# One level of Strassen's method in the first matrix product of a fused attention and gated-MLP kernel

## The chip, the cores and the metric

The kernel runs on one core of a Trainium2 chip. The metric is the device time of one execution in microseconds (us), taken as the median of several runs.

## The reference

For each of 4 batches there is a channel attention over 6080 tokens of 256 channels, and its output goes through an MLP of width 2048. In short (tau is 1.0):

```python
qn = q / (np.linalg.norm(q, axis=1, keepdims=True) + 1e-06)
kn = k / (np.linalg.norm(k, axis=1, keepdims=True) + 1e-06)
s = kn.transpose(0, 2, 1) @ qn / tau          # 256 x 256 per batch
a = softmax(s)
x = (v @ a).reshape(B * S, D)                 # 24320 tokens x 256
h = x @ w_in                                  # 2048 columns
g = h * (1.0 / (1.0 + np.exp(-1.702 * h)))
out = g @ w_out
```

q, k and v are float32; the weights w_in and w_out arrive as 64-bit floats and are turned into float32 on the chip.

## The kernel before

The attention matrix is folded into the weights: per batch W = a @ w_in (256 x 2048) is computed once, and the first product is v @ W. Every float32 operand of a large product is held as two tiles of a rounded format (F32R), a high part and a low part: `split` (lines 77-80) makes the high part with a copy on ACT (the cast of line 78) and the low part with a subtraction on DVE (line 79). One product is three matmuls: high by high, high by low, low by high.

A batch has 12 chunks of tokens: 11 of 512 and one of 448. W has 16 blocks of 128 columns (f = 0 to 15). For each chunk and each block, `hidden` (line 456) makes h for 128 columns and 512 tokens: two halves of the 256 channels (j) times three matmuls, so 6 matmuls of 512 columns into one PSUM bank `ps_h` (line 466). ACT takes the gate out of PSUM (line 473, tile g), makes gh (line 78), and DVE makes gl (line 79). Two to three steps later `project` (line 484) multiplies by w_out: 2 halves of the output times 3 matmuls, again 6 matmuls of 512 columns (line 494), summed over the 16 blocks in two PSUM banks `ps_o`. One step of the loop over (chunk, block) is thus 12 matmuls.

Between the steps lies other work, given by a table of due steps (`put`, lines 641-689): the next chunk of v is loaded and split (`v_load`, `v_split`, tiles v_h and v_l); the next batch's q and k are split (qs, ks), squared and summed for the norms (sq on ACT, acc on POOL, lines 240-243) and multiplied to scores (lines 288 and 297, the latter matmuls of 256 columns) every four steps; and before a batch ends its W is made (`weights`, line 406, four groups of four blocks). In the first batch w_in and w_out are also converted (lines 121-135) while two chunks run side by side. PE's order is written out by hand; the other engines' order comes from a scheduler, and each engine then works through its queue strictly in that order.

## Time and profile before

| what | value |
|---|---|
| time, 3 runs | 2280.66 us median (2280.4 to 2280.85) |
| the profiled execution's own time | 2280.42 us |
| its span in the profile | 2278.6 us |
| PE (matmul) | busy 2272.3 us, 100% of the span, 10256 matmuls |
| ACT | busy 1233.9 us, 54% |
| DVE | busy 904.8 us, 40% |
| POOL | busy 221.0 us, 10% |

A row of the groups by line reads: line, engine, operation, tile written <- tiles read, shape, count, then busy us and mean ns of one, then the idle time of the engine ahead of them and who ended it. In the timeline a row gives start, duration, engine, line and operation; xN merges N instructions. Matmuls are pipelined, so a matmul's duration is longer than the distance to the next one: the distance of two starts is what a matmul costs in a row.

### The profile page before, as it was taken

To read this page: it belongs to the slowest core of one execution; us is meant where nothing else is said; L and a number is where in the kernel's file an instruction comes from. 1 tells how busy PE (TensorE), PEld (TensorE's weight loads), DVE (VectorE), ACT (ScalarE), POOL (GpSimd) and SP (SyncE) were. 2 spreads that over 40 slices of the span, in tenths; PEclk is the share of its full clock that TensorE was granted. 3 is DMA by queue.
4 is the path that set the end of the run, shared out by engine and by line. 5 is a ranking of instruction groups with operands and counts; after the bars stand their busy time and mean duration, and the time that the engine had idled before them with its cause. 6 is when DMAs were issued, how large, how long until landed. Compare 5 with 4: busy or idle time off the path is not lost.

```text
span 2278.6 us, 26628 instructions
## 1 busy us (share of the span) xinstructions
PE 2272.3 (100%) x10256; PEld 1902.0 (83%) x10256; DVE 904.8 (40%) x1305; ACT 1233.9 (54%) x2146; POOL 221.0 (10%) x168
## 2 busy tenths in 40 slices
PE   9999999999999999999999999999999999999999
PEld 8888888888888888888888888888888888888888
DVE  7754444433334444443333444444333223223222
ACT  7765555554455555555545555555454445444444
POOL 0022222000002222200000222220000000000000
PEclk9999999999999999999999999999999999999999
DMA  9312111100011211110000121210001000000000
GB/s 367 93 47 65 65 56 54 56 18 19 20 36 56 74 56 56 63 47 18 19 28 27 61 70 56 66 44 19 18 19 36 19 19 32 25 19 29 27 10 18
DMA packets 45520, 109.72 MB, mean 48 GB/s; under 512 B 4432, under 2 KB 7248, under 8 KB 45392
## 3 DMA queue, kind: packets, MB, share of 16 engines
q1 hardware_dynamic: 45392, 108.02, 14.1%
q8 instruction: 80, 1.31, 0.2%
q14 instruction: 48, 0.39, 0.1%
HBM read 83.10 MB, written 24.90 MB: 47 GB/s over the span
## 4 chain that ended last, share of the span: by engine, by line
PE 99%; DVE 0%; DMA 0%; SPq 0%; issue 0%; ACT 0%; DVEq 0%
PE ps_h L466 46%; PE ps_o L494 45%; PE s L288 3%; PE ps_w L420 2%; PE s L278 2%; PE s L297 1%; DMA raw_k<-in_k 0%; PE ps_n L315 0%; PE s_first L253 0%; SPq L207 0%; DVE v_l L85 0%; PE ps_t L392 0%; PE ps_b L340 0%; DVE wl L79 0%; DVE m L367 0%
## 5 line engine op out<-in xcount | busy, mean ns | idle before, releaser
L473 ACT ACTIVATE g<-ps_h 128x512 f32<-128x512 f32 (+1 forms) x768 | 455.6, 593 | 945.1 <-PE ps_h L466 937.7
L79 DVE TENSOR_TENSOR gl<-g,gh 128x512 fp32r<-128x512 f32 (+1 forms) x768 | 591.6, 772 | 942.0 <-ACT gh L78 941.7
L466 PE MATMUL ps_h<-v_h,wh 128*128 128x512 f32 (+1 forms) x1536 | 596.8, 389 | 0.0
L466 PE MATMUL ps_h<-v_l,wh 128*128 128x512 f32 (+1 forms) x1536 | 595.5, 388 | 0.0
L466 PE MATMUL ps_h<-v_h,wl 128*128 128x512 f32 (+1 forms) x1536 | 594.7, 387 | 0.2 <-DVE wl L79 0.2
L494 PE MATMUL ps_o<-gh,wo_l 128*128 128x512 f32 (+1 forms) x1536 | 594.7, 387 | 0.0
L494 PE MATMUL ps_o<-gh,wo_h 128*128 128x512 f32 (+1 forms) x1536 | 594.7, 387 | 0.0
L494 PE MATMUL ps_o<-gl,wo_h 128*128 128x512 f32 (+1 forms) x1536 | 594.5, 387 | 0.0
L78 ACT CAST gh<-g 128x512 fp32r<-128x512 f32 (+1 forms) x768 | 472.7, 615 | 20.5
L466 PEld LDWEIGHTS ps_h<-v_h,wl 128*128 128x128 f32 x1536 | 288.3, 188 | 58.2 <-DVE wl L79 0.6
L494 PEld LDWEIGHTS ps_o<-gh,wo_l 128*128 128x128 f32 x1536 | 288.4, 188 | 57.1
L494 PEld LDWEIGHTS ps_o<-gh,wo_h 128*128 128x128 f32 x1536 | 288.3, 188 | 57.1
L494 PEld LDWEIGHTS ps_o<-gl,wo_h 128*128 128x128 f32 x1536 | 288.3, 188 | 56.7
L466 PEld LDWEIGHTS ps_h<-v_h,wh 128*128 128x128 f32 x1536 | 288.7, 188 | 54.8
L466 PEld LDWEIGHTS ps_h<-v_l,wh 128*128 128x128 f32 x1536 | 288.7, 188 | 54.4
L243 POOL TENSOR_TENSOR acc_q<-acc_q,sq 128x512 f32<-128x512 f32 (+1 forms) x72 | 90.0, 1251 | 1245.9 <-ACT sq L241 1245.9
L79 DVE TENSOR_TENSOR qs<-raw_q,qs 128x512 fp32r<-128x512 f32 (+1 forms) x71 | 47.6, 670 | 212.8 <-ACT qs L78 210.0
L243 POOL TENSOR_TENSOR acc_k<-acc_k,sq 128x512 f32<-128x512 f32 (+1 forms) x72 | 117.8, 1636 | 0.2
L79 DVE TENSOR_TENSOR v_l<-v_raw,v_h 128x512 fp32r<-128x512 f32 (+1 forms) x92 | 65.1, 748 | 79.1 <-ACT v_h L78 79.1
L288 PE MATMUL s<-qs,ks 128*128 128x512 f32 x272 | 73.2, 389 | 0.0
L241 ACT ACTIVATE sq<-raw_k 128x512 f32<-128x512 f32 (+1 forms) x96 | 57.9, 604 | 6.2 <-DMA raw_k<-in_k 3.4
L241 ACT ACTIVATE sq<-raw_q 128x512 f32<-128x512 f32 (+1 forms) x96 | 58.8, 613 | 2.1 <-DMA raw_q<-in_q 2.1
(92 smaller groups left out, 860.2 us busy)
## 6 DMA issues: line engine op xcount, KB each, us to landing
v_raw<-in_vT SPq DMA_DIRECT2D x44, 512.0 KB, 3.8
out_T<-osb SPq DMA_DIRECT2D x88, 256.0 KB, 2.1
raw_q<-in_q SPq DMA_DIRECT2D x43, 512.0 KB, 3.7
raw_k<-in_k SPq DMA_DIRECT2D x43, 512.0 KB, 4.4
words<-in_w_in SPq DMA_DIRECT2D x8, 512.0 KB, 8.0
words<-in_w_out SPq DMA_DIRECT2D x8, 512.0 KB, 3.4
v_raw<-in_vT SPq DMA_DIRECT2D x4, 448.0 KB, 3.6
out_T<-osb SPq DMA_DIRECT2D x8, 224.0 KB, 2.0
```

The source lines that it names most:

```text
L78: ins = nc.scalar.copy(dst_hi, src)
L79: nc.vector.tensor_tensor(dst_lo, src, dst_hi.bitcast(F32), op=ALU.subtract)
L241: nc.scalar.activation(sq, r, AF.Square)
L243: eng.tensor_tensor(acc, acc, sq, op=ALU.add)
L278: nc.tensor.matmul(self.s[i][:, :C], lhsT=ks[:, j, i * P : (i + 1) * P], rhs=qs[:, j, :], start=u == start and j == 0, stop=last and j == ...
L288: nc.tensor.matmul(self.s[i], lhsT=ks[:, j, 0, i * P : (i + 1) * P], rhs=qs[:, j, :, :], start=u == start and j == 0, stop=False, skip_gro ...
L297: nc.tensor.matmul(self.s[i][:, C:], lhsT=ks[:, j, 1, i * P : (i + 1) * P], rhs=qs[:, j, 0, :], start=False, stop=last and j == nt - 1, sk ...
L420: nc.tensor.matmul(ps, lhsT=l[:, j, ci], rhs=r[:, j, :], start=n == 0, stop=n == 3 * NC2 - 1,)
L466: nc.tensor.matmul(ps[:, :w], lhsT=l[:, j, fs], rhs=r[:, j, :w], start=n == 0, stop=n == 3 * NC2 - 1,)
L473: newest[0] = nc.scalar.activation(g, ps[:, :w], AF.Gelu_apprx_sigmoid)
L494: nc.tensor.matmul(out[d][:, :w], lhsT=l[:, f, ds], rhs=r[:, :w], start=f == 0 and n == 0, stop=f == NF - 1 and n == 2,)
```

## The change

`hidden` becomes a class, `Hidden`, which works on a pair of blocks of W's columns (fp = 0 to 7) and on the two halves of a chunk (256 tokens each, 224 in the short chunk). With the two halves of the channels this is a 2 by 2 by 2 product of blocks: eight block products in the plain way, seven by Strassen's method (in Winograd's form). Each block product is three matmuls of 256 columns, so a pair of blocks takes 21 matmuls of 256 columns, where two calls of `hidden` took 12 of 512. `project` is unchanged.

The seven products need seven combinations of the blocks of W and of v. For v, `v_load` now makes three transfers, `v_sums` makes four sums or differences of 128x256 (on POOL, but on DVE for the first three chunks), and `v_split` splits seven parts of 256 columns (as 512, 512, 512 and 256) instead of two of 512. For W, the product is copied out of PSUM by ACT, `weight_sums` makes four sums (on POOL, in the first batch on DVE), and `weight_split` splits seven blocks instead of four.

The results are put together in two PSUM banks, ps_x and ps_y, in three stages. `begin`: two products; ACT copies the first to r1 (L553), DVE adds it to the second: u2 (L554). `middle`: two products; DVE adds r25 (L561) and then adds r25 into ps_y (L563). `end`: three products added into the banks; DVE adds u2 into ps_x (L569) and into ps_y (L570), then the two gates follow (L581) with gh and gl. In PE's order `end` of a pair comes right ahead of `begin` of the next: 15 matmuls of 256 columns, then a `project` of 6 of 512, then `middle` (6 of 256), then a `project` of 6 of 512, then the next `end`. By the waits in the built program the first matmul of `middle` waits for u2, its fourth for r1, the first of `end` for r25, and the seventh of `end` for the sum of L563.

Room is found by other means: ps_h has 4 banks and ps_o 2 (before 3 and 3), the float32 w_in goes to DRAM and is loaded again per group, the squares have 2 buffers instead of 4, and several tiles share room. The work between the steps has new due steps, and W of the next batch is made in the last chunk and the first steps after it.

```diff
-    ps_h = ctx.enter_context(tc.tile_pool(name="ps_h", bufs=3, space=PSUM))
-    ps_o = ctx.enter_context(tc.tile_pool(name="ps_o", bufs=3, space=PSUM))
+    ps_h = ctx.enter_context(tc.tile_pool(name="ps_h", bufs=4, space=PSUM))
+    ps_o = ctx.enter_context(tc.tile_pool(name="ps_o", bufs=2, space=PSUM))
...
-                    sq = sp.tile([P, UT, C], F32, tag="sq", name="sq", bufs=4)[:, :nt, :]
+                    sq = sp.tile([P, UT, C], F32, tag="sq", name="sq", bufs=2)[:, :nt, :]
...
+        def spare(self, i, name):
+            if self.alone:
+                return ps_h.tile([P, NCH], F32, tag="h", name=name)
+            return ps_s.tile([P, NCH], F32, tag=f"s{i}", name=name)
...
+        def win_load(self, g):
+            win[g] = sp.tile([P, NC2, GW], F32, tag="win", name="win", bufs=1)
+            nc.sync.dma_start(win[g], parts[g])
         def win_split(self, g, step=split):
             self.win_h = sp.tile([P, NC2, GW], F32R, tag="qs", name="win_h")
             self.win_l = sp.tile([P, NC2, GW], F32R, tag="ks", name="win_l")
-            return step(self.win_h, self.win_l, win[:, :, g * GW : (g + 1) * GW])
+            if self.alone:
+                parts[g] = dram.tile([P, NC2, GW], F32, name=f"win{g}")
+                nc.sync.dma_start(parts[g], win[g])
+            return step(self.win_h, self.win_l, win[g])
...
-            return split(self.wh[g][:, i, :], self.wl[g][:, i, :], ps)
...
+            src = ps.rearrange("p (q f n) -> p f q n", q=2, f=2)
+            for f in range(2):
+                nc.scalar.copy(self.wf[0][:, ((0, 3), (1, 2))[i][f]], src[:, f])
+        def weight_sums(self, g):
+            t, u = self.wf
+            eng = nc.vector if self.alone else nc.gpsimd
+            eng.tensor_tensor(u[:, 1], t[:, 0], t[:, 3], op=ALU.subtract)
+            eng.tensor_tensor(t[:, 3], t[:, 3], t[:, 2], op=ALU.add)
+            eng.tensor_tensor(u[:, 0], t[:, 3], t[:, 0], op=ALU.subtract)
+            eng.tensor_tensor(u[:, 2], t[:, 1], u[:, 0], op=ALU.subtract)
+        def weight_split(self, g, part):
+            if part == 0:
+                self.wh[g] = wp.tile([P, 7, 2, P], F32R, tag=f"wh{g}", name="wh")
+                self.wl[g] = wp.tile([P, 7, 2, P], F32R, tag=f"wl{g}", name="wl")
+            o = slice(*((0, 4), (4, 7))[part])
+            split(self.wh[g][:, o], self.wl[g][:, o], self.wf[part])
...
+        early = b == 0 and c < 2
+        room = [(wp, f"{t}{1 + c}") if early else (cv, "words") for t in ("wh", "wl")]
+        t, u = (
+            pool.tile([P, n, NCH // 2], F32, tag=tag, name="v_raw")
+            for n, (pool, tag) in zip((4, 3), room)
+        )
+        vraw[b, c] = (t, u)
+        src = vT[b, :, o : o + w].rearrange("(c p) (h n) -> p c h n", p=P, h=2)
+        nc.sync.dma_start(t[:, 1:3, :hw], src[:, 1])
+        nc.sync.dma_start(t[:, 0, :hw], src[:, 0, 0])
+        nc.sync.dma_start(t[:, 3, :hw], src[:, 0, 1])
+    def v_sums(b, c):
+        hw = chunks[c][1] // 2
+        t, u = (x[:, :, :hw] for x in vraw[b, c])
+        eng = nc.vector if b == 0 and c < 3 else nc.gpsimd
+        eng.tensor_tensor(u[:, 1], t[:, 2], t[:, 3], op=ALU.subtract)
+        eng.tensor_tensor(t[:, 3], t[:, 3], t[:, 0], op=ALU.subtract)
+        eng.tensor_tensor(u[:, 0], t[:, 2], t[:, 3], op=ALU.subtract)
+        eng.tensor_tensor(u[:, 2], t[:, 1], u[:, 0], op=ALU.subtract)
+    def v_split(b, c, part, step=split):
+        hw = chunks[c][1] // 2
+        if part == 0:
+            vparts[b, c] = [
+                vp.tile([P, 7, NCH // 2], F32R, tag=t, name=t) for t in ("vh", "vl")
+            ]
+        n = 4 if b == 0 and c < 2 else 2
+        o = slice(2 * part, min(2 * part + n, 7))
+        i = slice(2 * part % 4, 2 * part % 4 + (o.stop - o.start))
+        h, l = (x[:, o, :hw] for x in vparts[b, c])
+        return step(h, l, vraw[b, c][part // 2][:, i, :hw])
...
-    def hidden(at, b, c, f):
-        w = chunks[c][1]
-        vh, vl = vsplit[b, c]
-        grp, o = divmod(f, FG)
-        fs = slice(o * P, (o + 1) * P)
-        wh, wl = at.wh[grp], at.wl[grp]
-        ps = ps_h.tile([P, NCH], F32, tag="h", name="ps_h")
-        n = 0
-        for j in range(NC2):
-            for l, r in ((wh, vh), (wh, vl), (wl, vh)):
...
+    class Hidden:
+        def __init__(self, at, b, c, fp):
+            self.b, self.c, self.fp = b, c, fp
+            self.hw = chunks[c][1] // 2
+            self.w = [x[fp // 2][:, :, fp % 2, :] for x in (at.wh, at.wl)]
+            self.v = vparts[b, c]
+        def product(self, out, wi, vi, first=False, last=False):
+            (wh, wl), (vh, vl) = self.w, self.v
+            for n, (l, r) in enumerate(((wh, vh), (wh, vl), (wl, vh))):
                 nc.tensor.matmul(
-                    ps[:, :w], lhsT=l[:, j, fs], rhs=r[:, j, :w],
-                    start=n == 0, stop=n == 3 * NC2 - 1,
+                    out, lhsT=l[:, wi, :], rhs=r[:, vi, : self.hw],
+                    start=first and n == 0, stop=last and n == 2,
+                    skip_group_check=True,
                 )
-                n += 1
-        g = gp.tile([P, NCH], F32, tag="g", name="g")[:, :w]
-        newest[0] = nc.scalar.activation(g, ps[:, :w], AF.Gelu_apprx_sigmoid)
-        there = wide[0] and wide[0] % 5 < 2
-        gh = (cv if there else gp).tile([P, NCH], F32R, tag="z" if there else "gh", name="gh")
-        gl = (cv if there else gp).tile([P, NCH], F32R, tag="low" if there else "gl", name="gl")
-        wide[0] += wide[0] > 0
-        split(gh[:, :w], gl[:, :w], g)
-        return gh, gl
+        def begin(self):
+            hw = self.hw
+            x, y = (ps_h.tile([P, NCH], F32, tag="h", name=nm) for nm in ("ps_x", "ps_y"))
+            self.x = x[:, : 2 * hw].rearrange("p (h n) -> p h n", h=2)
+            self.y = y[:, : 2 * hw].rearrange("p (h n) -> p h n", h=2)
+            self.product(self.x[:, 0], 0, 0, first=True)
+            self.product(self.y[:, 1], 4, 4, first=True)
+            r1, u2 = (
+                gp.tile([P, NCH // 2], F32, tag=tag, name=nm, bufs=2)[:, :hw]
+                for nm, tag in (("r1", "r"), ("u2", "u2"))
+            )
+            self.u2 = u2
+            newest[0] = nc.scalar.copy(r1, self.x[:, 0])
+            nc.vector.tensor_tensor(u2, self.y[:, 1], r1, op=ALU.add)
+        def middle(self):
+            hw = self.hw
+            self.product(self.y[:, 0], 5, 5)
+            self.product(self.x[:, 1], 3, 3)
+            r = gp.tile([P, NCH // 2], F32, tag="r", name="r25", bufs=2)[:, :hw]
+            nc.vector.tensor_tensor(r, self.x[:, 1], self.u2, op=ALU.add)
+            nc.vector.tensor_tensor(self.y[:, 1], self.y[:, 0], r, op=ALU.add)
+        def end(self):
+            self.product(self.x[:, 0], 1, 1, last=True)
+            self.product(self.x[:, 1], 6, 2, last=True)
+            self.product(self.y[:, 0], 2, 6, last=True)
+            nc.vector.tensor_tensor(self.x[:, 1], self.x[:, 1], self.u2, op=ALU.add)
+            nc.vector.tensor_tensor(self.y[:, 0], self.y[:, 0], self.u2, op=ALU.add)
+            return [
+                (self.b, self.c, 2 * self.fp + n, *self.gate(ps))
+                for n, ps in enumerate((self.x, self.y))
+            ]
...
+        def gate(self, ps):
+            w = 2 * self.hw
+            ps = ps.rearrange("p h n -> p (h n)")
+            g = gp.tile([P, NCH], F32, tag="g", name="g", bufs=2)[:, :w]
+            nc.scalar.activation(g, ps, AF.Gelu_apprx_sigmoid)
...
+            for s, (c, fp) in enumerate(order):
+                if b == 0 and 2 * s == WIDE:
+                    wide[0] = 1
+                if open_:
+                    late.extend(open_.pop().end())
+                h = Hidden(at, b, c, fp)
+                open_.append(h)
+                h.begin()
+                if len(late) > 2:
+                    project(*late.pop(0))
+                sides(2 * s)
+                h.middle()
+                if len(late) > 2:
+                    project(*late.pop(0))
+                sides(2 * s + 1)```

The order on two engines at a seam between chunks shows what the scheduler made of it. On ACT, before, the splitting of v (v_h) stands between a gate and its gh, in the last batch:

```order
L473 ACTIVATE g<-ps_h 128x512
L78 CAST v_h<-v_raw 128x512 x2
L78 CAST gh<-g 128x512
L473 ACTIVATE g<-ps_h 128x512
L78 CAST gh<-g 128x512
```

After, at the same seam (r_... is r1 of a pair, ps_x and ps_y are its two banks):

```order
L553 COPY r_24263<-ps_x 128x256
L581 ACTIVATE g<-ps_y 128x512
L82 CAST gh<-g 128x512 x2
L82 CAST vh<-v_raw 128x512 x3
L82 CAST vh<-v_raw 128x256
L581 ACTIVATE g<-ps_x 128x512
L553 COPY r_24321<-ps_x 128x256
L581 ACTIVATE g<-ps_y 128x512
```

The four casts of v now stand ahead of the gate of a pair's ps_x and of the next pair's r1. By the waits in the built program, the first of them waits for the last matmul of `end` of the last pair of the chunk whose vh and vl are overwritten (there are two buffers of each).

On DVE, before:

```order
L79 TENSOR_TENSOR gl<-g,gh 128x512 x13
L79 TENSOR_TENSOR v_l<-v_raw,v_h 128x512 x2
L79 TENSOR_TENSOR gl<-g,gh 128x512 x3
L502 COPY osb<-ps_o 128x512
L79 TENSOR_TENSOR gl<-g,gh 128x512 x13
```

After, the two pairs around the same seam (u_... is u2, r_... beside ps_x is r25 or r1):

```order
L554 TENSOR_TENSOR u_24264<-ps_y,r_24263 128x256
L83 TENSOR_TENSOR gl<-g,gh 128x512 x2
L561 TENSOR_TENSOR r_24281<-ps_x,u_24264 128x256
L563 TENSOR_TENSOR ps_y<-ps_y,r_24281 128x256
L569 TENSOR_TENSOR ps_x<-ps_x,u_24264 128x256
L570 TENSOR_TENSOR ps_y<-ps_y,u_24264 128x256
L83 TENSOR_TENSOR vl<-v_raw,vh 128x512 x3
L83 TENSOR_TENSOR vl<-v_raw,vh 128x256
L554 TENSOR_TENSOR u_24322<-ps_y,r_24321 128x256
L83 TENSOR_TENSOR gl<-g,gh 128x512
```

DVE has six kinds of work in a pair where it had one, and at the seam the four subtractions of v stand between a pair's last sum and the next pair's u2. Such a group of four stands on both engines once per chunk, 46 times in the program.

More of the change, by code (lines that the diff above doesn't have):

```diff
@@ L178, in __init__ @@
             short = UT if self.alone else 0
-            self.loads = [(t, RT) for t in range(short, T + 1, RT)]
+            self.rt = 6 if self.alone else RT
+            self.loads = [(t, self.rt) for t in range(short, T + 1, self.rt)]
             if short:
@@ L387, in transposes @@
             self.aT_l = small.tile([P, NC2, C], F32R, tag="aT_l", name="aT_l")
-            ps = ps_h.tile([P, NCH], F32, tag="h", name="ps_t")
+            ps = self.spare(0, "ps_t")
             psv = ps.rearrange("p (c x) -> p c x", c=NC2)
@@ L611, in channel_attention_then_glu @@
     for s, (what, n) in begun.items():
-        if s > 2:
+        if (what, n) not in (("in", 3), ("out", 1)):
             put0(s - 3, fetch[what], n)
```

174 lines of the change are left out of this document (95 added, 79 removed).

## The prediction

> **What bounds the kernel now.** I read the page first: the busy shares, the granted clock and the chain that ended last.
>
> ```profile
> span 2278.6 us, 26628 instructions
> PE 2272.3 (100%) x10256; PEld 1902.0 (83%) x10256; DVE 904.8 (40%) x1305; ACT 1233.9 (54%) x2146; POOL 221.0 (10%) x168
> PEclk9999999999999999999999999999999999999999
> PE 99%; DVE 0%; DMA 0%; SPq 0%; issue 0%; ACT 0%; DVEq 0%
> PE ps_h L466 46%; PE ps_o L494 45%; PE s L288 3%; PE ps_w L420 2%; PE s L278 2%; PE s L297 1%; DMA raw_k<-in_k 0%; PE ps_n L315 0%; PE s_first L253 0%; SPq L207 0%; DVE v_l L85 0%; PE ps_t L392 0%; PE ps_b L340 0%; DVE wl L79 0%; DVE m L367 0%
> ```
>
> PE is the bound in every stage, at full clock, and half of its time is the product that the change rewrites. So any matmul time saved there is saved from the end, unless PE then has to wait. What a matmul costs in a row is the distance of two starts; the timeline of PE beside a score step of batch 1 shows both sizes.
>
> ```profile
> 880.08 0.39 PE L466 MATMUL ps_h<-v_h,wh 128*128 128x512 f32 x1
> ...
> 885.30 0.39 PE L494 MATMUL ps_o<-gh,wo_l 128*128 128x512 f32 x1
> 885.52 1.07 PE L288 MATMUL s<-qs,ks 128*128 128x512 f32 x4
> 886.43 0.64 PE L297 MATMUL s<-qs,ks 128*128 128x256 f32 x4
> 886.90 0.40 PE L466 MATMUL ps_h<-v_h,wh 128*128 128x512 f32 x1
> ...
> 888.06 0.39 PE L466 MATMUL ps_h<-v_h,wl 128*128 128x512 f32 x1
> ```
>
> From 880.08 to 885.52 lie the 24 matmuls of two steps: 5.44 us, 0.227 each. The four of 256 columns take 886.43 to 886.90: 0.1175 each, not half of 0.227. And the five of 512 that follow them take 888.06 - 886.90 = 1.16, 0.232 each: a little is given back after a run of short ones.
>
> **The matmuls: what goes and what comes.** For a pair of blocks, 24 matmuls of 512 (5.44) become 21 of 256 and 12 of 512 in two runs of six. 21 x 0.1175 = 2.47; each run of six is five at 0.232 and one at 0.227, 1.39, twice 2.77. The pair takes 5.24: 0.20 less. There are 4 x 11 x 8 = 352 such pairs, 70 us. The 32 pairs of the short chunks scale about as their columns, 0.18 each, 6 us. Sum: -76 us. The bounds: four short ones are few, and 0.47 is rounded, so 0.12 may stand for 0.1175 (21 x 0.0025 = 0.05 a pair, -57 us in all); if nothing is given back after them (0.227 all through), 0.05 more, -95 us.
>
> The Trainium skill, "TensorE: Matmul & The Clock Gate", section "Back-to-back issue gap", puts the warm distance at N/2.4 + 2.5 ns: 109 ns for 256 columns and 216 for 512. By that a pair would save 12 x 216 - 21 x 109 = 0.30 us, an estimate of 115 us in all; this trace disagrees on both sizes (0.1175 and 0.227), and the rows decide.
>
> **Whether PE can keep that pace.** Before, ACT and DVE only waited for PE. Now PE waits for them four times a pair, so I walk through a pair by hand. Durations come from the groups by line and shape, distances on one engine from the timeline.
>
> ```profile
> L79 DVE TENSOR_TENSOR gl<-g,gh 128x512 fp32r<-128x512 f32 x704 | 551.7, 785 | 850.1 <-ACT gh L78 849.8
> L297 PE MATMUL s<-qs,ks 128*128 128x256 f32 x272 | 43.7, 281 | 0.0
> L297 PEld LDWEIGHTS s<-qs,ks 128*128 128x128 f32 x272 | 42.0, 189 | 5.5
> L79 DVE TENSOR_TENSOR win_l<-win,win_h 128x1024 fp32r<-128x1024 f32 x15 | 19.2, 1277 | 6.6 <-ACT win_h L78 6.6
> L78 ACT CAST win_h<-win 128x1024 fp32r<-128x1024 f32 x15 | 15.7, 1049 | 1.6 <-PE s L297 0.8 <-DVE win L135 0.7
> L361 DVE TENSOR_TENSOR x<-s,x 128x256 f32<-128x256 f32 x6 | 2.3, 417 | 0.7 <-ACT x L360 0.7
> L360 ACT COPY x<-s 128x256 f32<-128x256 f32 x4 | 1.3, 376 | 1.4 <-PE s L297 1.4
> ```
>
> ```profile
> 1002.21 0.39 PE L466 MATMUL ps_h<-v_h,wl 128*128 128x512 f32 x1
> ...
> 1002.64 0.60 ACT L473 ACTIVATE g<-ps_h 128x512 f32<-128x512 f32 x1 [1.47 <-PE ps_h L466]
> ...
> 1003.27 0.62 ACT L78 CAST gh<-g 128x512 fp32r<-128x512 f32 x1
> ...
> 1003.92 0.69 DVE L79 TENSOR_TENSOR gl<-g,gh 128x512 fp32r<-128x512 f32 x1 [2.03 <-ACT gh L78]
> ...
> 1005.36 0.60 ACT L473 ACTIVATE g<-ps_h 128x512 f32<-128x512 f32 x1 [1.47 <-PE ps_h L466]
> ...
> 1005.85 1.13 ACT L78 CAST v_h<-v_raw 128x512 fp32r<-128x512 f32 x2
> ...
> 1006.49 1.30 DVE L79 TENSOR_TENSOR v_l<-v_raw,v_h 128x512 fp32r<-128x512 f32 x2 [1.88 <-ACT v_h L78]
> ...
> 1006.88 0.62 ACT L78 CAST gh<-g 128x512 fp32r<-128x512 f32 x1
> ```
>
> A gate takes 0.60, a cast 0.62, a subtraction of 512 0.69; whoever waits starts 0.03 to 0.04 after the end. Work that needn't wait starts earlier: the next cast 0.49 after a gate (1005.36, 1005.85), 0.515 after a cast (two in 1.03), the next subtraction 0.61 after one (1.30 - 0.69); I take 0.1 off a copy and 0.08 off an add in the same way, 0.27 and 0.33. A sum out of PSUM of 256 is L361, 0.417; r1 is L360, 0.376; a matmul of 256 ends 0.28 after its start.
>
> Count from the first matmul of `end` of the pair before. `end` lasts 1.06, `begin` until 1.76, `project` until 3.15: there `middle` is due. It lasts until 3.86, the second `project` until 5.24: there the next `end` is due. L569 can start at 0.91 (its product's last start 0.59, and 0.28 + 0.04), L570 at 1.26. ACT: gate of ps_x 1.37, r1 1.86 to 2.24, gate of ps_y 2.13, gh 2.62 to 3.24 and 3.14 to 3.76. DVE: u2 2.27 to 2.69, so `middle` is met with 0.4 to spare; gl 3.27 and 3.88, r25 4.49 to 4.91 (its product is done at 4.06), so `end` is met with 0.3 to spare; L563 until 5.36, due only at 5.95. An ordinary pair keeps PE's pace.
>
> **The seam between chunks.** It doesn't, by the same walk, where v is split. The first cast of vh waits for the last matmul of `end`: 1.26. Then ACT has the casts at 1.26, 1.78, 2.29 and 2.81, the gate at 3.08 and r1 at 3.57 to 3.95. DVE's four subtractions stand at 1.91, 2.52, 3.13 and 3.74, then u2 from 4.07 to 4.49. `middle` is due at 3.15 and can start at 4.53: 1.38 late. Either queue alone makes it late (r1 alone: u2 at 3.98). Before, nobody on PE waited for what is queued behind these casts. What a wait costs beyond itself shows where PE waits for a weight split in the first steps:
>
> ```profile
> 59.42 0.50 PE L466 MATMUL ps_h<-v_h,wl 128*128 128x512 f32 x1 [0.15 <-DVE wl L79]
> 59.76 0.40 PE L466 MATMUL ps_h<-v_h,wh 128*128 128x512 f32 x1
> ```
>
> The next one comes 0.34 later, not 0.23: 0.11 more. So 1.49 a seam; 45 of the 46 groups lie outside the first steps: +67 us. Bounds: 1.28 if only r1 is late (58), 1.9 if the subtractions also meet POOL (86).
>
> **The other added work.** *POOL beside DVE.* The subtractions are slower while POOL works:
>
> ```profile
> 890.79 1.29 POOL L243 TENSOR_TENSOR acc_q<-acc_q,sq 128x512 f32<-128x512 f32 x1 [9.29 <-ACT sq L241]
> 891.71 0.92 DVE L79 TENSOR_TENSOR gl<-g,gh 128x512 fp32r<-128x512 f32 x1 [0.78 <-ACT gh L78]
> 892.04 1.73 POOL L243 TENSOR_TENSOR acc_k<-acc_k,sq 128x512 f32<-128x512 f32 x1
> 892.86 1.47 DVE L79 TENSOR_TENSOR gl<-g,gh 128x512 fp32r<-128x512 f32 x1 [0.23 <-ACT gh L78]
> ```
>
> 0.92 and 1.47 instead of 0.69. Where the next batch's q and k are prepared (every second pair, 68 times by the 272 matmuls of L297), ACT's two casts and two squares push gh to 4.70; a gl of 1.47 then ends at 6.82, and the following sums and u2 at 8.44, where `middle` is due at 8.39: 0.1 late, 0.2 with the restart. Where the gl takes 0.69 nothing is late. v's four sums on POOL add such a meeting once a chunk, 0 to 0.3. Together 0 to 27 us; I take 12. The Trainium skill, "SBUF — State Buffer", section "Who interferes with whom", says that a DVE instruction contends with a POOL read only if both its inputs are in SBUF, so the new sums out of PSUM would be spared; no row here has one beside POOL.
>
> *W of the next batch*, 12 groups: 1.75 times the split, in `win_h`-sized pieces (1.05 on ACT, 1.28 on DVE) beside the gates. The walk gives u2 about 0.5 late once a group, with the restart 0.6: +7, between 0 and 18.
>
> *The first 16 pairs*, where DVE also converts the weights:
>
> ```profile
> 58.00:75.00 17.00, 16.85 (x75) 13.63 (x74) 15.08 (x26) 12.52 (x22) 0.00 (x0) 1.00 0.30 94
> 75.00:97.00 22.00, 22.00 (x98) 18.19 (x97) 15.61 (x27) 15.91 (x27) 0.00 (x0) 1.00 0.31 96
> 97.00:120.00 23.00, 23.00 (x103) 18.97 (x101) 16.39 (x27) 15.96 (x27) 0.00 (x0) 1.00 0.31 92
> 120.00:146.00 26.00, 26.00 (x116) 21.48 (x115) 13.10 (x21) 16.97 (x31) 2.53 (x2) 1.00 0.00 1
> ```
>
> DVE (fourth figure of time) works 60 of these 88 us. Added are 80 sums of 0.417 (33), three groups of W (4 sums and 0.75 of a split more, 7) and one group of v (2): 102, less 0.08 for each of some 200 neighbours, 86 at best. So DVE is full there, and PE gains nothing: I take 98, +10 against the 88, between -3 and +20; the 3 us of savings that the sum counts for them are within that.
>
> *Before the first product* the new path from W in PSUM is two copies (0.65), three sums in a row (1.35), a cast of 1.05 and a subtraction of 1.28, 4.3, against 0.6 + 0.7: +3, between 0 and 6. At the end, the last two gates lie behind four `project`s' worth of matmuls as before: nothing.
>
> **Sum.** -76 + 67 + 12 + 7 + 10 + 3 = +23 on the profiled execution's 2280.42 (its span 2278.6 and 1.8 around it; 0.24 under the median of 2280.66): 2303 us. With all terms at their ends the case reaches from 2240 (-95 + 58 - 3) to 2380 (-57 + 86 + 27 + 18 + 20 + 6).
>
> **Rivals.** *The seam is hidden (faster).* Both engines have room (DVE 40%, ACT 54%), and the walk fails at one place only. If `middle` isn't held there, 67 us go: 2236. It decides as soon as a seam costs under (76 - 32)/45 = 0.98 us. Against it: two queues, each late by itself.
>
> *Long runs of short matmuls are cheaper than four of them (faster).* At half of 0.227, a pair saves 12 x 0.227 - 21 x 0.1135 = 0.34, 131 us with the short chunks as full ones: 2280 - 131 + 99 = 2248. Against it: the four measured. The Trainium skill's distances of 109 and 216 ns ("TensorE: Matmul & The Clock Gate", "Back-to-back issue gap") would give 2280 - 115 + 99 = 2264, an estimate.
>
> *The chain of an ordinary pair is late (slower).* The spare 0.3 ahead of r25 is small: sums that read and write PSUM at 0.6 instead of 0.417, or gl at its mean of 0.785 instead of 0.69, use it up. At 0.2 to 0.3 a pair it costs 77 to 115 more, about 2400.
>
> *Weight loads set the pace of long runs (slower).* A load is 0.189 long. At that pace 21 take 3.97, 1.50 more a pair, 576 us: 2880. Against it: in the run of four the loads overlap.
>
> **Chances.** The forecast's case 0.61 (0.08 of it within 0.2%, 2276 to 2285, about what a measurement of this kernel can tell from no change; 0.53 above); the hidden seam 0.19; cheaper short matmuls 0.04; the late chain 0.11; weight loads 0.03; anything else slower 0.02. Faster 0.23, same 0.08, slower 0.69. The likeliest case's own range is 2258 to 2352. The range goes down to 2236, the middle of the first rival: left out are half of it, the late chain's greater part and the weight loads.
>
> **What would show it.** In the profile after: matmuls of L535 at 0.117 to 0.12 from start to start; PE's idle time, now near zero, some 100 us, its largest part ahead of ps_y at L535 and put down to u2 (L554), once a chunk, 1.4 us each; DVE at 9 tenths in the slices up to 150 us. It is wrong if PE is idle in every pair (late chain), or at no seam (hidden), or if the distance inside a run of short ones is not 0.12.

## The result, and the profile after

| | us, median | range |
|---|---|---|
| before (same chip, 4 runs) | 2280.76 | 2280.4 to 2281.04 |
| after (4 runs) | 2376.78 | 2373.77 to 2378.41 |

The ratio is 1.042 (95% interval 1.0402 to 1.0438): slower by 96 us, where +23 was forecast. The direction held, the size didn't: 2376.78 lies above the range's upper end of 2352. The page of the profiled execution after (its span, busy time by engine, the granted clock in 40 slices, the chain that ended last):

```profile
span 2374.8 us, 36966 instructions
...
PE 2266.9 (95%) x13712; PEld 2001.5 (84%) x13712; DVE 1667.0 (70%) x3347; ACT 1329.7 (56%) x2690; POOL 390.4 (16%) x396
...
PEclk9899999999999999999999999999999999999999
...
PE 73%; DVE 12%; ACT 10%; issue 4%; DMA 1%; SPq 0%; ACTq 0%; DVEq 0%
```

PE was 99% of the chain and is 73%: for 22% of the span the chain now runs through DVE and ACT. PE's idle time is 2374.8 - 2266.9 = 108 us, near the forecast ("some 100 us"). That is luck in part: the losses measured further below add up to 146 us, because a wait shows shorter than it costs (1.20 us at a seam that costs 1.47) and PE counts as busy while its clock is low. The slice of the clock that reads 8 is new. Who holds PE (waits of PE, then of its weight loads: us in total, times, longest):

```profile
PE ps_y L535 <- DVE u L554: 77.4, 65, 4.0
PE ps_x L535 <- DVE r L561: 5.1, 3, 3.4
PE ps_y L535 <- DVE ps_y L563: 4.9, 10, 0.6
PE ps_t L409 <- DVE x L394: 3.3, 1, 3.3
```

```profile
PEld ps_y L535 <- DVE u L554: 123.2, 103, 4.4
```

The wait foreseen, `middle` for u2, is the largest by far. Forecast was 45 times; here it is 65 times, at most 4.0 us instead of 1.4, and a weight load is held up 103 times. The seam itself, at the start of a chunk of the last batch (first row: the first matmul of `end` of the pair before):

```profile
2018.87 0.28 PE L535 MATMUL ps_x<-vh,wh 128*128 128x256 f32 x1
...
2020.14 1.97 ACT L82 CAST vh<-v_raw 128x512 fp32r<-128x512 f32 x4 [2.73 <-PE ps_y L535]
...
2020.79 2.23 DVE L83 TENSOR_TENSOR vl<-v_raw,vh 128x512 fp32r<-128x512 f32 x4 [0.22 <-ACT vh L82]
...
2022.50 0.36 ACT L553 COPY r<-ps_x 128x256 f32<-128x256 f32 x1
...
2022.94 0.42 DVE L554 TENSOR_TENSOR u<-ps_y,r 128x256 f32<-128x256 f32 x1
...
2023.41 0.39 PE L535 MATMUL ps_y<-vh,wh 128*128 128x256 f32 x1 [1.20 <-DVE u L554]
2023.63 0.28 PE L535 MATMUL ps_y<-vl,wh 128*128 128x256 f32 x1
```

Counted from 2018.87, the walk of the prediction had u2 at 4.07 and `middle` at 4.53; here they start at 4.07 and 4.54, and the matmul behind comes 0.22 later instead of 0.12. At 31 seams the interval from one `end` to the next is 6.73 to 6.76 us, 1.47 more than the 5.28 of an ordinary pair (forecast 1.49); at seven more it is 6.51 to 6.69.

The pace of PE in its runs, where nothing waits:

```profile
2244.04 0.28 PE L535 MATMUL ps_x<-vl,wh 128*128 128x256 f32 x1
2244.16 0.28 PE L535 MATMUL ps_x<-vh,wl 128*128 128x256 f32 x1
2244.28 0.40 PE L602 MATMUL ps_o<-gh,wo_h 128*128 128x512 f32 x1
...
2245.67 0.28 PE L535 MATMUL ps_x<-vh,wh 128*128 128x256 f32 x1
```

0.12 a short one, and 1.39 for six of 512. Over all pairs the medians are 0.713 for a run of 6 short ones, 1.793 for 15, and 1.388 for six long ones: a pair takes 0.713 + 1.793 + 2 x 1.388 = 5.28 us, and some 200 of the 383 intervals from one `end` to the next take just that (with other matmuls between them, such as those of q and k, taken off). An ordinary pair keeps PE's pace, as the walk said; but the pace is 5.28, not 5.24.

What else was lost, and was priced too low, shows at three places. The first is where q and k of the next batch are prepared, in every second pair. In batches 2 and 3 three of the four such pairs of a chunk lose 0.34 us; the one right behind a seam loses nothing:

```profile
847.77 1.36 POOL L254 TENSOR_TENSOR acc_q<-acc_q,sq 128x512 f32<-128x512 f32 x1 [9.68 <-ACT sq L252]
...
848.43 0.43 DVE L563 TENSOR_TENSOR ps_y<-ps_y,r 128x256 f32<-128x256 f32 x1
...
849.08 1.29 POOL L254 TENSOR_TENSOR acc_k<-acc_k,sq 128x512 f32<-128x512 f32 x1
849.23 1.69 DVE L83 TENSOR_TENSOR gl<-g,gh 128x512 fp32r<-128x512 f32 x1 [0.37 <-ACT gh L82]
```

gl takes 1.69 beside POOL, where the prediction took at most 1.47 from the trace of before. The second place is the turn of a batch, where the last weights' casts and subtractions meet the seam:

```profile
669.13 1.97 ACT L82 CAST vh<-v_raw 128x512 fp32r<-128x512 f32 x4 [0.27 <-PE ps_y L535]
...
669.90 1.46 DVE L83 TENSOR_TENSOR wl<-wf,wh 128x1024 fp32r<-128x1024 f32 x1
...
671.59 2.22 DVE L83 TENSOR_TENSOR vl<-v_raw,vh 128x512 fp32r<-128x512 f32 x4
...
673.73 0.94 DVE L83 TENSOR_TENSOR wl<-wf,wh 128x768 fp32r<-128x768 f32 x1
...
674.60 0.41 DVE L554 TENSOR_TENSOR u<-ps_y,r 128x256 f32<-128x256 f32 x1
...
675.06 0.39 PE L535 MATMUL ps_y<-vh,wh 128*128 128x256 f32 x1 [4.04 <-DVE u L554]
```

u2 stands behind both: PE waits 4.04 us here, and 4.02 and 4.04 at the other two turns; two groups of W ahead of each turn cost 1.29 each. The third place is the first pairs. In windows of time the columns are length, then busy time and count of PE, PEld, DVE, ACT and POOL, then the granted clock:

```profile
66.00:75.00 9.00, 5.40 (x30) 3.78 (x28) 8.76 (x17) 5.44 (x10) 0.00 (x0) 1.00 0.26 65
75.00:86.00 11.00, 8.21 (x31) 7.09 (x31) 10.93 (x24) 8.28 (x15) 0.00 (x0) 0.53 0.67 232
86.00:98.00 12.00, 10.78 (x62) 9.05 (x61) 11.19 (x24) 7.67 (x16) 0.00 (x0) 1.00 0.14 46
```

DVE is full, as forecast (8.76 of 9 us, 10.93 of 11, 11.19 of 12), but the clock fell to 0.53 in the middle window, which nothing in the trace of before suggested.

### The profile page after: what moved, and what is told of

Its sections match the earlier page's. It is cut to its first block, busy times and chain, and to the rows that moved or that the text cites. A ratio compares the mean times of both kernels' runs of the same rounds, so it can differ in the third digit from the quotient of the medians.

```text
span 2374.8 us, 36966 instructions
## 1 busy us (share of the span) xinstructions
PE 2266.9 (95%) x13712; PEld 2001.5 (84%) x13712; DVE 1667.0 (70%) x3347; ACT 1329.7 (56%) x2690; POOL 390.4 (16%) x396
## 4 chain that ended last, share of the span: by engine, by line
PE 73%; DVE 12%; ACT 10%; issue 4%; DMA 1%; SPq 0%; ACTq 0%; DVEq 0%
PE ps_o L602 33%; PE ps_x L535 19%; PE ps_y L535 14%; DVE gl L83 3%; ACT vh L82 3%; PE s L299 3%; ACT g L581 2%; PE ps_w L448 2%; DVE ps_x L569 2%; DVE u L554 1%; PE s L308 1%; DVE vl L83 1%; DVE ps_y L570 1%; DVE wl L83 1%; ACT gh L82 1%
## 5 line engine op out<-in xcount | busy, mean ns | idle before, releaser
L83 DVE TENSOR_TENSOR gl<-g,gh 128x512 fp32r<-128x512 f32 (+1 forms) x768 | 567.3, 760 | 167.2 <-ACT gh L82 162.5
L602 PE MATMUL ps_o<-gl,wo_h 128*128 128x512 f32 (+1 forms) x1536 | 605.1, 394 | 0.8 <-DVE gl L83 0.7
L602 PE MATMUL ps_o<-gh,wo_h 128*128 128x512 f32 (+1 forms) x1536 | 605.9, 394 | 0.0
L602 PE MATMUL ps_o<-gh,wo_l 128*128 128x512 f32 (+1 forms) x1536 | 597.2, 389 | 0.0
L581 ACT ACTIVATE g<-ps_x 128x512 f32<-128x512 f32 (+1 forms) x384 | 227.6, 593 | 652.0 <-DVE ps_x L569 651.5
L82 ACT CAST gh<-g 128x512 fp32r<-128x512 f32 (+1 forms) x768 | 443.7, 627 | 4.3 <-PE ps_o L602 0.7
L535 PE MATMUL ps_x<-vh,wh 128*128 128x256 f32 (+1 forms) x1536 | 435.2, 283 | 5.4 <-DVE r L561 5.1
L535 PE MATMUL ps_x<-vl,wh 128*128 128x256 f32 (+1 forms) x1536 | 434.5, 283 | 1.5 <-DVE vl L83 1.5
L535 PE MATMUL ps_x<-vh,wl 128*128 128x256 f32 (+1 forms) x1536 | 434.6, 283 | 0.7 <-DVE wl L83 0.7
L535 PE MATMUL ps_y<-vh,wh 128*128 128x256 f32 (+1 forms) x1152 | 340.9, 296 | 87.0 <-DVE u L554 77.4
L569 DVE TENSOR_TENSOR ps_x<-ps_x,u 128x256 f32<-128x256 f32 (+1 forms) x384 | 163.9, 427 | 269.0 <-PE ps_x L535 266.9
L535 PEld LDWEIGHTS ps_y<-vh,wh 128*128 128x128 f32 x1152 | 219.8, 191 | 148.9 <-DVE u L554 123.2
L602 PEld LDWEIGHTS ps_o<-gh,wo_l 128*128 128x128 f32 x1536 | 290.2, 189 | 62.1
L535 PE MATMUL ps_y<-vh,wl 128*128 128x256 f32 (+1 forms) x1152 | 325.9, 283 | 2.6 <-DVE wl L83 2.6
L535 PE MATMUL ps_y<-vl,wh 128*128 128x256 f32 (+1 forms) x1152 | 325.7, 283 | 0.2 <-DVE vl L83 0.2
L602 PEld LDWEIGHTS ps_o<-gh,wo_h 128*128 128x128 f32 x1536 | 292.7, 191 | 34.4
L602 PEld LDWEIGHTS ps_o<-gl,wo_h 128*128 128x128 f32 x1536 | 292.4, 190 | 31.9 <-DVE gl L83 1.8
L535 PEld LDWEIGHTS ps_x<-vh,wh 128*128 128x128 f32 x1536 | 293.9, 191 | 26.2 <-DVE r L561 12.1
L535 PEld LDWEIGHTS ps_x<-vl,wh 128*128 128x128 f32 x1536 | 294.2, 192 | 12.8 <-DVE vl L83 1.7
L535 PEld LDWEIGHTS ps_x<-vh,wl 128*128 128x128 f32 x1536 | 294.3, 192 | 0.9 <-DVE wl L83 0.9
L554 DVE TENSOR_TENSOR u<-ps_y,r 128x256 f32<-128x256 f32 (+1 forms) x384 | 160.5, 418 | 151.6 <-ACT r L553 150.5
L581 ACT ACTIVATE g<-ps_y 128x512 f32<-128x512 f32 (+1 forms) x384 | 231.5, 603 | 0.4 <-DVE ps_y L570 0.4
```

The source lines that it names most:

```text
L82: ins = nc.scalar.copy(dst_hi, src)
L83: nc.vector.tensor_tensor(dst_lo, src, dst_hi.bitcast(F32), op=ALU.subtract)
L535: nc.tensor.matmul(out, lhsT=l[:, wi, :], rhs=r[:, vi, : self.hw], start=first and n == 0, stop=last and n == 2, skip_group_check=True,)
L554: nc.vector.tensor_tensor(u2, self.y[:, 1], r1, op=ALU.add)
L569: nc.vector.tensor_tensor(self.x[:, 1], self.x[:, 1], self.u2, op=ALU.add)
L581: nc.scalar.activation(g, ps, AF.Gelu_apprx_sigmoid)
```

## The experiments

Theory A, put forward after this comparison: nothing is short of capacity after the first pairs; PE waits because r1 and u2, on which it depends within a pair, stand in strict queues behind work that could wait (the splits of v and W, a slow gl). Theory B, its rival: ACT and DVE are too full, and a wait removed at one place comes back at another. Every time is a median, and its ratio is to the kernel before on the same chip; since that kernel took 2280.43 to 2280.76 us on all chips used, the times are also compared with 2376.78, the kernel after.

**1. The splits of v held back.** `pinned` holds an instruction back, in the scheduler's order, behind the newest r1.

```diff
-                    put(at_v + 8 + 2 * n if first_v == at_v + 3 else 29 + n // 2, v_split, *bc, n)
+                    put(at_v + 8 + 2 * n if first_v == at_v + 3 else 29 + n // 2, pinned, v_split, *bc, n)
```

> The changed kernel with one difference: the four splits of the next chunk's v are held back on ACT and DVE until r1 of the pair at whose step the program issues them, so that the scheduler can't pull them forward to the seam. All work stays. Theory A (order: at a seam u2 is late only because vh and vl stand ahead of r1 and u2 in their queues): the 45 waits of 1.4 to 1.5 us go (66 us), and of the three waits of 4.0 us at the turn of a batch the part that v makes (2.5 each); a split behind r1 and ahead of gl may cost up to 0.2 us in a pair that also prepares q and k (4 times a chunk, at most 20 us). Time 2300 to 2325, PE's idle time 30 to 50 us instead of 108. Theory B (capacity: ACT and DVE are too full around the split, the late work only moves to other pairs): 2355 to 2380, with new waits of the same sum before ps_y in the middle of the chunks.

Measured: 2320.93 (ratio 1.0178, 1.0163 to 1.0193), 56 us less than after. Waits of PE:

```profile
PE ps_o L602 <- DVE gl L83: 16.8, 26, 0.9
PE ps_y L535 <- DVE u L554: 15.7, 25, 1.3
PE ps_x L535 <- DVE r L561: 8.2, 11, 3.4
```

The wait for u2 fell from 77.4 to 15.7 us with every instruction still there: it was the order. But a new wait came, 16.8 us for gl, which now stands behind vl; a pair with both a split and q and k takes 6.3 where it took 5.62. Part of it came back, as B has it, and the time stays 22 us above that of the next run.

**2. No work on v at all.**

```diff
-            for c in range(2 if b == 0 else 1, NCHUNK + (b + 1 < B)):
+            for c in range(1, NCHUNK + 1):
+                vparts[divmod(b * NCHUNK + c, NCHUNK)] = vparts[0, 1 if (b, c) == (0, 1) else 0]
+            for c in ():
```

> The changed kernel with the loads, the sums on POOL and the splits of v left out from the third chunk on: all later chunks multiply the split v of the first chunk, so the output is that of another v. This prices all that the change does for v outside the first steps. Theory A: 66 us for the seams, 7 us for the waits two pairs behind them where POOL works on v's sums, 7 us of the long waits at the turns: 2295 to 2305. If the run with the splits held back comes within 12 us of this one, it was the place of the splits in the queues that cost, not the work. Theory B (the seam waits have another cause, the change of PSUM buffers between chunks or the output's copies): the waits before ps_y at the seams stay, 2355 to 2377.

Measured: 2298.45 (1.0079, 1.0064 to 1.0094): 78 us for all that v costs outside the first steps, as A has it. The first run came within 22 us of it, not within 12: of the 78, 56 were the splits' place, and 22 stayed with their work and the sums on POOL.

**3. No sums on DVE between the products.**

```diff
             newest[0] = nc.scalar.copy(r1, self.x[:, 0])
-            nc.vector.tensor_tensor(u2, self.y[:, 1], r1, op=ALU.add)
...
-            nc.vector.tensor_tensor(r, self.x[:, 1], self.u2, op=ALU.add)
-            nc.vector.tensor_tensor(self.y[:, 1], self.y[:, 0], r, op=ALU.add)
...
-            nc.vector.tensor_tensor(self.x[:, 1], self.x[:, 1], self.u2, op=ALU.add)
-            nc.vector.tensor_tensor(self.y[:, 0], self.y[:, 0], self.u2, op=ALU.add)
```

> The changed kernel with the five sums of each pair on DVE left out (u2, r25 and the three into PSUM; r1 is still copied): the seven products run in the same order into the same buffers, each gate reads what the products left there, so the output isn't the product. PE then waits for nothing inside a pair, and what is left is the pace of 21 matmuls of 256 and 12 of 512. Theory A (long runs of short matmuls go at 0.120 us, and a pair takes 5.28): 2280.4 - 60 + 8 (the first product later) + 0 to 8 (what is left of the first pairs' waits) = 2228 to 2238. Theory B (the sizes of the prediction, 0.1175 and 5.24 a pair, and the rest of the lost time lies in the sums): 2210 to 2222. If time beyond 2250 is left, something other than the sums holds PE.

Measured: 2307.09 (1.0111, 1.0096 to 1.0126); both forecasts missed, because PE found another to wait for:

```profile
PE ps_x L535 <- ACT r L553: 50.0, 48, 3.3
```

With DVE out of it, r1 alone holds `middle` at the seams, 1.04 us a time, behind the four casts of vh. This bears out the prediction's "either queue alone makes it late" for ACT's queue, by a run that was meant to show something else. The size can't be set against the walk's 1.28: PE waits here at the fourth matmul of `middle` and not at the first, and at the seam looked into (2033 to 2041 us) a cast of gh stands between those of vh and r1.

**4. Short matmuls alone, in the kernel before.**

```diff
-                nc.tensor.matmul(
-                    ps[:, :w], lhsT=l[:, j, fs], rhs=r[:, j, :w],
-                    start=n == 0, stop=n == 3 * NC2 - 1,
-                )
+                for h in (0, 1):
+                    hs = slice(h * w // 2, (h + 1) * w // 2)
+                    nc.tensor.matmul(
+                        ps[:, hs], lhsT=l[:, j, fs], rhs=r[:, j, hs],
+                        start=n == 0 and h == 0, stop=n == 3 * NC2 - 1 and h == 1,
+                        skip_group_check=True,
+                    )
```

> The kernel before with each matmul of its first product cut into two of half the columns, same operands, same sums: 24 matmuls of 256 and 12 of 512 for two blocks instead of 24 of 512. It prices the short matmul without any wait of the change. By 0.120 us each and 1.388 for each run of six of 512 (what the changed kernel's trace shows) two blocks take 5.66 instead of 5.44: 352 x 0.22 + 32 x 0.2 = 84 us more, 2365. By the 0.1175 that the prediction took: 5.60, 61 us more, 2341. If a short one is half of a long one and nothing is given back: 2281 to 2285.

Measured: 2356.22 (1.0332, 1.0315 to 1.0349), +75.8. The trace has 12 short ones in 1.433 (0.113, 0.119, then 0.120 each) and six long ones in 1.387, 2.820 a block against 2.72: 0.100 x 768 = 77. The 84 of the expectation had taken 0.120 for the first two as well. So a short matmul costs 0.119 on the mean of a run, 5% above half of 0.227, and each run of six long ones behind it loses 0.027 more.

**5. Sums and r1 left out:** the third run's edit, and the copy r1 gone (what was held back behind r1 is now held back behind the newest matmul of a product).

```diff
-            newest[0] = nc.scalar.copy(r1, self.x[:, 0])
```

> The changed kernel with the five sums on DVE and the copy r1 on ACT left out, so the output isn't the product: PE runs the 21 + 12 matmuls of each pair with nothing to wait for inside it. (The run that left only the sums out still waited 48 times for r1, 1.04 us each, because its copy stands behind the four casts of vh: 50 us of its time.) Theory A (what is left is the pace, 5.28 a pair, and the later start): 2280.4 - 60 + 8 + 0 to 10 = 2228 to 2238. Theory B (PE is also held by something else that the change adds): over 2250, and then the waits of this run name it.

Measured: 2262.79 (0.9922, 0.9907 to 0.9937), 25 above the band of A and above the 2250 that speak for B. The place is plain, though. Windows of this run:

```profile
56.00:104.00 48.00, 29.46 (x110) 23.77 (x111) 39.20 (x54) 27.44 (x49) 17.36 (x12) 0.75 0.40 132
104.00:145.00 41.00, 37.36 (x214) 32.72 (x213) 36.28 (x65) 30.62 (x56) 0.00 (x0) 0.96 0.32 103
145.00:600.00 455.00, 453.78 (x2821) 408.48 (x2820) 189.70 (x281) 247.81 (x470) 92.58 (x85) 1.00 0.15 48
```

From 145 us on PE is busy 453.8 of 455, and a pair takes 5.28. Before that, without a single sum inside a pair, PE works 67 of 89 us, at a clock of 0.75 in the first half, and the first product comes at 70.5 us, where it came at 65.8 in the changed kernel. So the pace is A's, and the start loses time for reasons that this run doesn't separate. Even with all waits inside pairs gone the change is worth only 18 us here.

**6. No additions on POOL for q and k.**

```diff
-                    eng = nc.vector if self.alone else nc.gpsimd
-                    eng.tensor_tensor(acc, acc, sq, op=ALU.add)
+                    if self.alone:
+                        nc.vector.tensor_tensor(acc, acc, sq, op=ALU.add)
```

> The changed kernel without the additions on POOL that gather the squares of q and k for the batches after the first (L254; the norms are then wrong, the squares on ACT stay). In the changed kernel the pairs that prepare q and k take 5.62 instead of 5.28 in batches 2 and 3, 0.23 more in batch 1, 25 us in all, and a subtraction gl there took 1.70 us beside POOL instead of 0.69. Theory A (POOL beside DVE makes gl slow, and u2 behind it late): all 25 us go, 2348 to 2356. Theory B (ACT's two casts and two squares make r1 and the gates late, POOL's part is small): 2368 to 2377, and those pairs still take over 5.5.

Measured: 2354.88 (1.0326, 1.0311 to 1.0342), 22 us less than after, close to A's 25. The row for the weight loads of `middle`:

```profile
PEld ps_y L535 <- DVE u L554: 102.2, 68, 4.4
```

103 waits became 68 and 123.2 us became 102.2: 35 waits and 21 us were POOL's meeting with gl, though ACT's casts and squares are all still there.

**7. `end` issued behind the next `begin`.** No instruction changes, only PE's order: u2 gets the 1.06 us of `end` as room. The scheduler works out the order on the other engines anew, so the run shows both together.

```diff
-                if open_:
-                    late.extend(open_.pop().end())
                 h = Hidden(at, b, c, fp)
-                open_.append(h)
                 h.begin()
+                if open_:
+                    late.extend(open_.pop().end())
+                open_.append(h)
```

> The changed kernel with one difference: on PE `end` of a pair is issued behind `begin` of the next instead of ahead of it. The same instructions on every engine; u2 then has 1.06 us (the nine matmuls of `end`) more until `middle` needs it, r25 has the 0.70 us of `begin` more until `end` needs it, and the gates have that much less until their PSUM is wanted by the `begin` after the next. Theory A (PE waits only because r1 and u2 have too little room in a pair): the seam's 1.38 shrinks to 0.3 to 0.4, the pairs with q and k lose nothing, the waits of 1.3 at W's groups become small, and only the first pairs (DVE full, 24 us) and the later start (8) stay: 2376.8 - 45 x 1.05 - 25 - 12 to 20 = 2285 to 2295. Theory B (ACT and DVE are at their capacity; the wait moves to `begin`, for the gate two pairs before): 2340 to 2400.

Measured: 2297.46 (1.0075, 1.006 to 1.009), 79 us less than after, 2.5 above A's band and far from B. Waits of PE:

```profile
PE ps_y L535 <- DVE ps_y L563: 10.9, 16, 1.5
PE ps_y L535 <- DVE u L554: 10.8, 15, 1.2
PE ps_y L535 <- ACT g L581: 4.8, 3, 2.3
```

In the last batch a seam now costs nothing, because r1 comes ahead of the casts of vh in ACT's queue. In batches 2 and 3 a seam still costs 1.74, with q, k and vh in one pair.

**8. Both edits.**

> Both edits together: `end` issued behind the next `begin`, and the four splits of v held back behind r1 of the pair at whose step they are issued. Theory A: the seams and the pairs with q and k cost nothing, one late split is hidden by the new room: 2228 (the pace and the later start) + 24 (the first pairs) + 5 to 15 (softmax of batch 1 and W's groups) = 2255 to 2268, faster than the kernel before by about 1%. Theory B (capacity): over 2300, like the run that holds back the splits alone, with waits before ps_x or ps_y for a gate.

Measured: 2272.76 (0.9963, 0.9949 to 0.9977): faster than before, by 8 us, 4.8 above A's band. The seams and the pairs with q and k are at 5.28 nearly everywhere in batches 2 to 4; nine pairs at the turns lose 0.98, and a pair at each of the three softmaxes 3.85.

**9. The first batch's weights for all batches.**

```diff
-                for g in range(NG):
+                for g in ():
...
             if b + 1 < B:
+                nxt.wh, nxt.wl = at.wh, at.wl
                 at = nxt
```

> The changed kernel without the weights W of the batches after the first: they use the first batch's, so the output is that of other weights. Left out are 12 groups of work (loads, casts, subtractions, sums on POOL, copies, and on PE 144 matmuls of 512 that took 0.233 each, 33.6 us). What goes beyond these 33.6 us is the price of W in waits. Theory A (the W groups' casts and subtractions stand in the same queues ahead of r1 and u2, at the turn of a batch together with v's): the pairs at the turns of batches lost 32 us, of which three ordinary seams (4.4) stay, so 2376.8 - 33.6 - 28 = 2312 to 2319. Theory B (the size of the prediction, 0.6 a group): 2376.8 - 33.6 - 7 = 2333 to 2339.

Measured: 2321.78 (1.018, 1.0165 to 1.0195): 55.0 less than after, 33.6 of it matmuls. W's waits are worth 21 us: between the two forecasts, and three times the prediction's 7. The pairs of 6.07 ahead of the turns fell to 4.78, and the turns, 10.0, 10.7 and 10.5, to 6.5: 6 x 1.29 + 3.5 + 4.2 + 4.0 = 19.

**10. Less conversion of w_out.**

```diff
     def wout_convert(u):
+        if u:
+            r = words.pop(("out", u))[..., 1].bitcast(F32)
+            fs = slice(2 * u, 2 * u + 2)
+            nc.scalar.copy(wo_h[:, fs, :], r)
+            for _ in range(4):
+                yield
+            nc.scalar.copy(wo_l[:, fs, :], r)
+            yield
+            yield
+            return
```

> The changed kernel with the conversion of w_out from the second unit on cut down to two copies on ACT of the raw upper words, without the five instructions on DVE (0.42, 0.42, 0.68, 0.68 and 0.68 us by the trace, 2.9 a unit, 7 units, 20 us of DVE in the first twelve pairs); the second weights are then no weights. In the changed kernel the first 13 pairs took 89 us where 13 x 5.28 are 68.6: 20 us lost. Theory A (DVE is full there): most of it goes, 2376.8 less 12 to 18, 2359 to 2365. Theory B (the chain to the first weights, a transfer or the granted clock holds those pairs, not DVE's load): 2369 to 2377.

Measured: 2370.59 (1.04, 1.0383 to 1.0417), 6 us less than after: B, although 20 us of DVE's work were gone. But the pairs between the turns of weight groups did fall to 5.28: 85 us for the first 13 instead of 89.

**11. The tenth run, and less conversion of w_in.**

```diff
+        if g:
+            r = words.pop(("in", n))[..., 1].bitcast(F32)
+            nc.scalar.copy(win[g][:, c, :], r)
+            yield
+            yield
+            yield
+            return
         yield from to_float32(win[g][:, c, :], words.pop(("in", n)), [P, GW])
```

> As the run with the light conversion of w_out, and the conversion of w_in from the second group on cut down in the same way to one copy on ACT of the upper words (four instructions of DVE gone, 2.2 us for each of six half groups, 13 us more; the weights are then no weights). With w_out alone the pairs between the turns of the first four weight groups fell to 5.28, but the first two pairs (7.9 and 11.9) and the pairs at a new group (7.5 each) stayed long: 85 us for the first 13 instead of 89. Theory A (DVE's load: with w_in gone too the new groups come in time): the first 13 pairs take 70 to 76, 2356 to 2363. Theory B (the chain from w_in over the split, PE, ACT's copies, the sums and the split to the first matmul that needs a group is as long as before, and the first two pairs wait for the start's own work): 80 to 86, 2366 to 2372.

Measured: 2368.56 (1.038, 1.0363 to 1.0397), 8 us less than after: B again, the first 13 pairs at 81 us. What is left of the waits of PE from 50 to 150 us:

```profile
PE ps_t L426 <- DVE x L411: 3.6, 1, 3.6
PE ps_y L552 <- DVE wl L83: 2.5, 3, 1.1
PE ps_y L552 <- DVE u L571: 1.8, 2, 1.5
PE ps_x L552 <- DVE vl L83: 1.5, 1, 1.5
```

With 33 us of DVE's work gone the 13 pairs lost 12 us instead of 20: DVE's load was 8 of them. The rest goes with chains that are as long as before: softmax to the transposes, and wl three times, at the first pair that needs a new group.

**12. The best version tried:** both edits of the eighth, W's splits held back too, and the two Exp of a softmax kept together.

```diff
-                    put(total - NF + 4 * g + 2, nxt.win_split, g)
+                    put(total - NF + 4 * g + 2, pinned, nxt.win_split, g)
...
-                    put_w(n + 2, nxt.weight_split, g, 0)
-                    put_w(n + 2, nxt.weight_split, g, 1)
+                    put_w(n + 3, pinned, nxt.weight_split, g, 0)
+                    put_w(n + 3, pinned, nxt.weight_split, g, 1)
...
+            if self.alone:
+                exps()
+            else:
+                with tc.issue_after(gated[0].ins):
+                    exps()
```

> `end` behind the next `begin` and v's splits held back, as in the run that was faster than before, and two more edits: the splits of W and of w_in for the next batch are held back behind r1 too (W's one step later), and the two Exp of a softmax are held behind the gates that the program issued before them, so that no gate lies between two loads of ACT's tables. In the run without these edits nine pairs at W's groups lost 0.98 each and the pair of each softmax 3.85. Theory A: W's nine waits fall to 0.3 or less (6 us), and the softmax of at least two batches loses 1 instead of 3.85 (6 us): 2272.8 - 12 = 2257 to 2264. Theory B (these waits come from the amount of work in those pairs): 2268 to 2276.

Measured: 2258.22 (0.9903, 0.9889 to 0.9918), in A's band: 22 us faster than before and 119 faster than after, with the same work on every engine. Its page:

```profile
PE 2227.3 (99%) x13712; PEld 2003.9 (89%) x13712; DVE 1684.0 (75%) x3347; ACT 1340.9 (59%) x2690; POOL 421.5 (19%) x396
...
PE 94%; DVE 3%; ACT 2%; issue 1%; DMA 1%; SPq 0%; DVEq 0%; ACTq 0%
```

DVE and ACT are busier than in the changed kernel (75 and 59%), and PE is the bound again. So after the first pairs it was the order and not the capacity that cost: A. W's nine waits are gone; the two Exp came together in two of the three softmaxes (6.3 instead of 9.1 for that pair).

## Why the prediction was right in direction and wrong in size

| step of the prediction | forecast, us | measured, us | by |
|---|---|---|---|
| matmuls, 5.44 to 5.24 a pair | -76 | -59 | pair of 5.28; the short chunks 4.87 to 4.78 |
| the seam, 45 times | +67 | +66 | 45 x 1.47, as at the 31 seams |
| POOL beside DVE, q and k | +12 with v's sums | +22 | run 6 |
| v's sums | in the 12 | +7 | pairs two behind a seam |
| W of the next batch | +7 | +21 | run 9 |
| the first 16 pairs | +10 | +17 | 105 against 88, without their seam |
| the first product | +3 | +8 | 57.8 before, 65.8 after |
| the first softmax beside the products | not in the sum | +5 | one wait of 3.4, and the pair behind |

The measured column adds up to +87, where the kernel lost 96. Of the 9 us between them 3 are savings in the first 16 pairs, which both the first row and the row of these pairs contain. About 6 are not assigned; 2.5 of these show at the two later softmaxes, in pairs of 5.52 and 6.31.

*The seam was right*, in mechanism, place and size (runs 1 to 3), and an ordinary pair does keep PE's pace. The rivals "hidden seam", "weight loads" and "late chain in every pair" are refuted by the same rows; the runs of matmuls in this trace go at 120 ns for 256 columns and 227 to 236 for 512. The Trainium skill ("TensorE: Matmul & The Clock Gate", "Back-to-back issue gap") gives N/2.4 + 2.5 ns for the gap of a matmul by itself, 109 and 216 ns; this trace disagrees with both.

*The steps that failed are terms of the sum that were sized too low, all to the same side.*

- The matmuls, "21 x 0.1175 = 2.47": four matmuls between two rounded starts gave 0.1175; the 21 of a pair take 0.713 + 1.793 = 2.51, 0.1193 each. The saving is 59 us and not 76. The prediction had this bound (0.12) and chose the other.
- W, "The walk gives u2 about 0.5 late once a group": 7 us, and 21 by run 9. The walk followed one group through an ordinary pair. It never put the last groups and the seam into one queue, where PE waited 4.04 us.
- POOL, a gl of 1.47 that makes u2 "0.1 late, 0.2 with the restart": gl takes 1.69 and the pair loses 0.34; q and k alone cost 22 us by run 6, where 12 were allowed together with v's sums. Each of the 34 gl of 1.7 us in batches 2 and 3 lies beside one of q's and k's additions on POOL, as the one of 1.47 did; why it takes 1.69 here stays open.
- The first pairs were costed as DVE's load alone, 10 us, and lost 17; runs 10 and 11 show that load to be 8 of the 20 us that the first 13 pairs lose against a pace of 5.28.
- The first product, 3 us, was costed as the new path from W alone, and came 8 later. The path was sized well: from W's last matmul to the first product 2.67 us instead of 0.47, 2.2 more. Put at nothing was the rest: the transposes behind the softmax come at 57.02 instead of 52.87, and W's twelve matmuls, at a clock of 0.50 from 58.26 to 61.67, take 3.86 from first to last start instead of 2.75.

*The range failed with them.* The bounds of the terms reached to 2380, which holds the result; the range stopped at 2352 as if some of the terms would come out low. The waits of W, of q and k and of v's sums had a common cause, too little room ahead of u2, and so they went up together.

Left open: how the other 12 us of the first 13 pairs divide between the chains to the weights and the fallen clock. The distances in the slow stretch (last section) put about 3 of them to the clock, but no run changed the one without the other.

## What to carry to other kernels

When a change gives the busiest engine something to wait for, write down what can stand in the strict queues ahead of the awaited instruction at the busiest place, with all tables' work that falls due there, not at an ordinary step; and expect that terms with one cause miss together. A change that cuts work on the bound engine but ties it to others can lose for want of room alone: reordering PE by one stage and holding back splits moved this one from 4.2% slower to 1% faster, with the same work on every engine. And a price for a run of 15 matmuls should come from a run of that kind: a run of four, of which the first two come quicker, misjudges it.
